# Two exponent operations and three rounding operations moved later in the first head pair of a fused attention and feed-forward kernel

## The chip, the cores and the metric

One core of one Trainium2 chip. The time is the device time of one execution in microseconds (us). Executions of one kernel scatter by 1 to 2 us here, so small differences are judged on several runs beside runs of the kernel before on the same chip.

Engines by their short names: PE is TensorE (matmuls), PEld its weight loads, DVE VectorE, ACT ScalarE, POOL GpSimd, SP SyncE, which issues most loads. L171 is line 171 of the kernel.

## The reference

Attention with a hashed mask over 4 x 8 heads of 768 positions and 64 features, followed by a feed-forward block on the result. Cut to what matters:

```python
q_bits = (np.einsum('bhsd,dk->bhsk', q, proj) > 0)      # likewise k_bits
mask = q_bucket[:, :, :, None] == k_bucket[:, :, None, :]
scores = np.where(mask, scale * q @ k.T, -1e9)
attn = softmax(scores) ; x = attn @ v                    # (cut, in words)
h = x @ w_in ; r = np.maximum(h, 0) ; out = (r * r) @ w_out
```

The two weights of the feed-forward block arrive in float64 (a float32 array times a float64 scalar). The kernel has to make float32 of them itself, and does so with integer operations, 512 columns of 128 rows at a time, between the steps of the attention. Such a chunk is called a piece; each pair of heads brings two.

## The kernel before

Heads are worked off in 16 pairs. For a pair, PE makes hash values of 64 features, ACT turns them into bits, PE makes scores for six tiles of keys, ACT their exponentials, DVE adds these up, and PE multiplies them with the values ("attend"). A piece of weights needs three steps on two engines:

```python
    def part_weight(i):                     # splitting, on DVE: L143, L147
        nc.vector.tensor_scalar(out=power, in0=high, ...)
        nc.vector.tensor_scalar(out=top, in0=high, ...)

    def place_power(i):                     # exponent operations, on ACT: L160, L161
        nc.scalar.activation(out=small, in_=power, func=ACTF.Relu, bias=excess)
        nc.scalar.activation(out=power, in_=small, func=ACTF.Copy, scale=2.0**23)

    def round_weight(i):                    # rounding, on DVE: L171, L176, L179
        nc.vector.scalar_tensor_tensor(out=power, in0=high, ..., in1=power, ...)
        ...                                 # two more of the same kind
```

The first of the three rounding operations reads what the second exponent operation wrote. The loop over pairs, cut to the steps that the argument touches, in program order. Each engine gets its own instructions in this order:

```python
        for pr in range(NP):
            a, b = 2 * pr, 2 * pr + 1       # the two pieces of this pair
            ...
            if more and pr > 0:
                for w in range(2):
                    features(pr + 1, w)     # DVE: transposes q and k of the next pair, L333
            if pr > 0:
                round_weight(b - 2)
            ...
            score(pr, 0); score(pr, 1)      # PE: scores; ACT: exponentials
            if pr > 0:
                finish(pr - 1, prepare if more else None)   # PE: next pair's hash (L346),
                                            # sums of the last (L455), attends, spread (L477)
            add_up(pr, 1)                   # DVE
            ...
            part_weight(a)
            score(pr, 2)
            if pr == 0:
                prepare()                   # hash and bits of pair 1
            score(pr, 3)
            ...
            place_power(a)
            attend(pr, 0); attend(pr, 1)
            for kt in (2, 3):
                add_up(pr, kt)              # DVE
            ...
            round_weight(a)
            part_weight(b)
            ...
            score(pr, 4); score(pr, 5)
            if pr == 0:
                weigh(1)                    # ACT: L382
            place_power(b)
            attend(pr, 2); attend(pr, 3)
            add_up(pr, 4); add_up(pr, 5)    # DVE
```

Scores, hashes and sums share three buffers of PE's output memory. So the fourth user in a row has to wait until the first one has been read.

## Time and profile before

| | before |
|---|---|
| time, median of the 6 runs at the change's measurement | 880.06 us (879.69 to 881.27) |
| PE busy, share of the span | 99% |
| DVE busy | 87% |
| PE idle in 21 to 26 us | 1.37 of 5.00 us |
| PE's wait for tile 4's exponential | 0.99 us |
| hash of pair 2 on PE | 1.48 us |

The profile prints a group of instructions on a line: start, length, engine, line and operation, what it writes and reads, how often, and in brackets what ended an idle time before it. Lines the prediction shows are not repeated. These are PE's in the first pair and at pair 2's hash, in the timeline of the kernel before:

```profile
22.99 0.40 PE L396 MATMUL st<-bits,bits 64*128 64x512 bf16 x2
23.20 1.04 PE L396 MATMUL st<-feat,feat 64*128 64x512 f32 x4
25.23 0.29 PE L396 MATMUL st<-bits,bits 64*128 64x256 bf16 x2 [0.99 <-ACT e L413]
...
31.44 0.60 PE L396 MATMUL st<-feat,feat 64*128 64x256 f32 x4
31.96 1.48 PE L346 MATMUL hash<-feat,projs 64*32 64x384 f32 x16
33.37 0.85 PE L455 MATMUL tot<-total,ones 128*32 128x384 f32 x8
...
36.79 0.26 PE L477 MATMUL xo<-both,picks 128*64 128x24 f32 x4
```

The bracket at 25.23 is the wait that the change is after. The hash at 31.96 starts without a gap behind the scores of 31.44, but lasts 1.48 us. The line at 36.79 is a handy milestone further on.

### The profile page before, as it was taken

What the parts mean: (1) busy time and instruction counts of PE and PEld (TensorE: products, weight loads), DVE (VectorE), ACT (ScalarE), POOL (GpSimd) and SP (SyncE); (2) the same over time, 40 slices, a digit from 0 to 9 for tenths busy, and PEclk for the clock granted to TensorE, in tenths of its full rate; (3) what the DMA queues carried; (4) which work ended last, traced back from release to release, by engine and by line L of the source; (5) the groups of instructions that cost most, each with busy time, mean ns of one, the idle gap of its engine ahead of it and who ended that gap; (6) DMA issues with size and microseconds to landing.
All of it is one profiled execution on the core that took longest, in us unless ns stands there. A gap on an engine that the chain in (4) does not pass through costs nothing.

```text
span 877.9 us, 12130 instructions
## 1 busy us (share of the span) xinstructions
PE 864.8 (99%) x4340; PEld 518.7 (59%) x4340; DVE 760.4 (87%) x1099; ACT 391.5 (45%) x673; POOL 107.0 (12%) x172
## 2 busy tenths in 40 slices
PE   8999999999999999999999999999999999999996
PEld 3444444444444444444688865556888755568885
DVE  5999999999999998888779968888889788888875
ACT  6988888888888852222211123332111233321110
POOL 2000000000000001554231011111000211110002
PEclk9999999999999999999999999999999999999998
DMA  9777967998788536999897764536756754355565
GB/s 176 142 149 134 233 153 156 188 253 225 179 176 225 156 105 213 299 267 283 292 353 239 181 160 168 173 118 222 285 151 187 167 165 155 124 167 154 158 175 105
DMA packets 224131, 167.09 MB, mean 190 GB/s; under 512 B 164448, under 2 KB 181344, under 8 KB 224064
## 3 DMA queue, kind: packets, MB, share of 16 engines
q1 hardware_dynamic: 189152, 87.19, 41.0%
q0 software_dynamic: 12528, 41.30, 15.2%
q10 hardware_dynamic: 22384, 37.76, 14.0%
q8 instruction: 36, 0.59, 0.3%
q14 instruction: 31, 0.25, 0.1%
HBM read 124.52 MB, written 41.68 MB: 189 GB/s over the span
## 4 chain that ended last, share of the span: by engine, by line
PE 95%; DVE 2%; ACT 1%; DMA 1%; issue 0%; ACTq 0%; DVEq 0%
PE acc L712 40%; PE st L396 17%; PE acc L931 16%; PE xo L438 14%; PE acc L884 6%; PE hash L346 2%; PE tot L455 1%; DVE total L428 1%; DMA k_nat<-in_k_dram 1%; ACT bits L356 1%; ACT e L413 0%; PE xo L477 0%; DVE x_t L493 0%; PE tp L309 0%; DVE recs L487 0%
## 5 line engine op out<-in xcount | busy, mean ns | idle before, releaser
L413 ACT ACTIVATE e<-st 128x1024 f32<-128x1024 f32 x192 | 145.1, 810 | 44.9 <-PE st L396 41.0
L396 PE MATMUL st<-feat,feat 64*128 64x512 f32 (+1 forms) x768 | 150.4, 483 | 0.0
L438 PE MATMUL xo<-e,v_nat 128*64 128x512 f32 (+1 forms) x768 | 134.8, 492 | 0.0
L712 PE MATMUL acc<-b,leaf 128*128 128x256 f32 x600 | 133.2, 379 | 0.7 <-issue 0.7
L712 PEld LDWEIGHTS acc<-b,leaf 128*128 128x128 f32 x600 | 113.8, 190 | 17.1 <-issue 1.7
L428 DVE TENSOR_TENSOR total<-total,e 128x1536 f32<-128x1536 f32 x64 | 112.4, 1757 | 8.2 <-ACT e L413 3.6
L438 PEld LDWEIGHTS xo<-e,v_nat 128*64 128x64 f32 x768 | 51.3, 136 | 82.2 <-issue 74.3
L931 PE MATMUL acc<-t_x,w_unit 128*128 128x512 f32 x192 | 90.2, 592 | 0.0
L396 PEld LDWEIGHTS st<-feat,feat 64*128 64x128 f32 x768 | 66.0, 188 | 33.0 <-issue 23.2
L712 PE MATMUL acc<-t,leaf 128*128 128x256 f32 x336 | 76.3, 380 | 0.0
L356 ACT ACTIVATE bits<-hash,lifts 32x384 bf16<-32x384 f32 x120 | 68.6, 572 | 2.3 <-PE hash L346 0.5
L712 PEld LDWEIGHTS acc<-t,leaf 128*128 128x128 f32 x336 | 63.6, 190 | 9.4 <-DVE t L516 0.5
L796 DVE SCALAR_TENSOR_TENSOR b<-h 128x512 f32<-128x512 f32 x96 | 65.7, 691 | 3.0
L396 PE MATMUL st<-bits,bits 64*128 64x256 bf16 (+1 forms) x384 | 63.1, 325 | 1.7 <-ACT e L413 1.2
L931 PE MATMUL acc<-x,w_unit 128*128 128x512 f32 x128 | 60.1, 592 | 0.0
L712 PE MATMUL acc<-x,w_unit 128*128 128x512 f32 x128 | 56.6, 594 | 0.0
L712 PE MATMUL acc<-b_t,leaf 128*128 128x256 f32 x240 | 53.8, 379 | 0.0
L931 PEld LDWEIGHTS acc<-t_x,w_unit 128*128 128x128 f32 x192 | 36.5, 190 | 28.9 <-issue 26.8
L719 ACT COPY two<-acc 128x256 f32<-128x256 f32 (+1 forms) x29 | 12.5, 431 | 87.9 <-PE acc L712 63.1
L719 ACT COPY one<-acc 128x256 f32<-128x256 f32 (+1 forms) x29 | 12.5, 431 | 85.1 <-PE acc L712 46.9
L712 PEld LDWEIGHTS acc<-b_t,leaf 128*128 128x128 f32 x240 | 45.5, 190 | 6.2
L396 PEld LDWEIGHTS <-bits 64*128 64x128 bf16 x384 | 23.5, 93 | 42.5 <-issue 38.4
(159 smaller groups left out, 1165.5 us busy)
## 6 DMA issues: line engine op xcount, KB each, us to landing
leaf<-w_out ACTq DMA_DIRECT2D x142, 256.0 KB, 3.1
w_unit<-w_in SPq DMA_DIRECT2D x16, 640.0 KB, 4.0
raw<-in_moe_w_in_dram SPq DMA_DIRECT2D x16, 512.0 KB, 5.6
raw<-in_moe_w_out_dram SPq DMA_DIRECT2D x16, 512.0 KB, 4.6
w_unit<-w_in SPq DMA_DIRECT2D x8, 896.0 KB, 8.1
w_out<-sums POOLq DMA_DIRECT2D x16, 448.0 KB, 6.8
sum<-w_in SPq DMA_DIRECT2D x16, 448.0 KB, 4.8
v_nat<-in_v_dram SPq DMA_DIRECT2D x16, 384.0 KB, 4.3
```

The costliest lines, as they stand in the source:

```text
L346: nc.tensor.matmul(out=banks[g * NR_B:(g + 1) * NR_B, h, 0:HS], lhsT=projs[rows], rhs=feat[pr, w][rows, c * HS:(c + 1) * HS], start=True, ...
L356: nc.scalar.activation(out=t[h * D:h * D + NR_B, c * HS:(c + 1) * HS], in_=hashed[pr, w][at, h, 0:HS], func=ACTF.Sign, scale=HUGE, bias=li ...
L396: nc.tensor.matmul(out=st[:, h, 0:hi - lo], lhsT=src[pr, 1][rows, key], rhs=src[pr, 0][rows, lo:hi], start=first, stop=not first,)
L413: nc.scalar.activation(out=e[:, :, lo:hi], in_=sts[i][:, :, 0:hi - lo], func=ACTF.Exp, scale=scale)
L428: nc.vector.tensor_tensor(out=totals[pr], in0=totals[pr], in1=weights[pr, kt][:, :, 0:S], op=ALU.add)
L438: nc.tensor.matmul(out=xo[h * D:(h + 1) * D, lo:hi], lhsT=nat[pr, "v_nat"][:, h, kt * D:(kt + 1) * D], rhs=weights[pr, kt][:, h, lo:hi], s ...
L455: nc.tensor.matmul(out=tot[g * 32:(g + 1) * 32, 0:HS], lhsT=ones, rhs=totals[pr][:, h, c * HS:(c + 1) * HS], start=True, stop=True,)
L712: nc.tensor.matmul(out=acc[to], lhsT=a(i), rhs=b(i), start=first and i == 0, stop=last and i == n - 1, skip_group_check=True,)
L719: nc.scalar.copy(out=t, in_=acc[of])
L796: nc.vector.scalar_tensor_tensor(out=out, in0=h, scalar=0.0, in1=h, op0=ALU.max, op1=ALU.mult)
L884: nc.tensor.matmul(out=out, lhsT=w[:, a], rhs=b, start=start, stop=stop, skip_group_check=True)
L931: nc.tensor.matmul(out=acc[to], lhsT=w[:, PLACE[a], f], rhs=bt[b](f), start=first and f == 0, stop=last and f == NFT // 2 - 1, skip_group_ ...
```

## The change

In the first pair the exponent operations of piece 0 stand ahead of the exponentials of tiles 4 and 5, which PE waits for. The change puts them behind those exponentials, and the rounding, which needs them, behind that. Other pairs are untouched. The whole diff:

```diff
             score(pr, 3)
             if more and pr > 0:
                 weigh(pr + 1)
-            place_power(a)
+            if pr > 0:
+                place_power(a)
             attend(pr, 0)
             attend(pr, 1)
@@
-            round_weight(a)
+            if pr > 0:
+                round_weight(a)
             part_weight(b)
@@
             score(pr, 5)
             if pr == 0:
                 weigh(1)
+                place_power(0)
+                round_weight(0)
             place_power(b)
             attend(pr, 2)
             attend(pr, 3)
```

## The prediction

> **What bounds the kernel now.** I read the page first: busy shares, slices and the chain of waits. Then I read the change's own place, the first pair of heads, in the timelines of ScalarE (ACT), VectorE (DVE) and TensorE (PE), and last the busy time by stretch, to see whether anything lost early can be won back. From the page, the busy shares, three of the forty slices' rows, and the chain by engine:
>
> ```profile
> PE 864.8 (99%) x4340; PEld 518.7 (59%) x4340; DVE 760.4 (87%) x1099; ACT 391.5 (45%) x673; POOL 107.0 (12%) x172
> ...
> PE   8999999999999999999999999999999999999996
> ...
> DVE  5999999999999998888779968888889788888875
> ...
> PEclk9999999999999999999999999999999999999998
> ...
> PE 95%; DVE 2%; ACT 1%; DMA 1%; issue 0%; ACTq 0%; DVEq 0%
> ```
>
> PE sets the time: 95% of the chain. A microsecond that PE stands still in the attention stage ends in the time, unless a later stall would have absorbed it. The busy time by stretch says whether there is one (columns: stretch, length, then busy PE, weight loads, DVE, ACT, POOL):
>
> ```profile
> 21.00:26.00 5.00, 3.63 (x26) 1.95 (x27) 3.08 (x4) 4.92 (x8) 0.00 (x0) 1.00 0.99 221
> ...
> 34.00:54.00 20.00, 20.00 (x152) 9.13 (x148) 18.83 (x23) 17.00 (x26) 0.00 (x0) 1.00 0.71 133
> 54.00:74.00 20.00, 20.00 (x154) 9.17 (x150) 18.56 (x22) 17.16 (x26) 0.00 (x0) 1.00 0.70 132
> ```
>
> From 34 us on PE is busy 20.00 of 20 us; there is no later stall to absorb anything. Its only idle time near the change lies in 21 to 26 us, where ACT is busy 4.92 of 5.00. DVE has about 1.2 us of slack per 20 us. The chain of waits in that place:
>
> ```profile
> 21.34 1.51 ACT e L413 x2
> 22.86 0.03 issue
> 22.88 0.73 ACT small L160
> 23.61 0.02 issue
> 23.64 0.63 ACT power L161
> 24.27 0.93 ACT e L413
> 25.19 0.04 issue
> 25.23 0.72 PE st L396 x6
> ```
>
> Here the two exponent operations (L160, L161, of weight piece 0) stand ahead of the exponentials of key tile 4, and PE waits for the first of those. That is the wait the change aims at. The work that the change will displace is seen on DVE:
>
> ```profile
> 22.89 1.76 DVE L428 TENSOR_TENSOR total<-total,e 128x1536 f32<-128x1536 f32 x1 [3.59 <-ACT e L413]
> 24.57 0.69 DVE L171 SCALAR_TENSOR_TENSOR power<-raw,power 128x512 uint32<-128x512 uint32 x1
> ...
> 26.50 0.42 DVE L143 TENSOR_SCALAR power<-raw 128x512 uint32<-128x512 uint32 x1
> ...
> 27.17 3.62 DVE L428 TENSOR_TENSOR total<-total,e 128x1536 f32<-128x1536 f32 x2
> 30.70 0.97 DVE L333 STREAM_TRANSPOSE feat<-q_nat 128x768 f32<-128x768 f32 x1
> 31.60 0.94 DVE L333 STREAM_TRANSPOSE feat<-k_nat 128x768 f32<-128x768 f32 x1
> ```
>
> DVE idles 3.59 us, but only until 22.89; from there it runs without a gap through rounding of piece 0 (24.57), splitting of piece 1 (26.50), two additions (27.17) and the transposes of pair 2 (30.70, 31.60). PE already waits for the last of these: its weight load for the second half of the hash has "[0.47 <-DVE feat L333]" at 32.59. The hash of pair 2 takes PE 1.41 us in the chain, that of pair 3 only 0.81, so DVE is already 0.6 us late there.
>
> **What the Trainium skill says.** "Perfetto Trace Analysis", section "Tensor Engine Instruction (MATMUL, LD_WEIGHTS)": ACT and DVE are strict FIFO; only PE can pull weight loads ahead. So a DVE instruction that waits for ACT holds up everything behind it on DVE. The trace agrees: the timelines of both keep the program's order throughout, and DVE's 3.59 us wait was spent with the additions for tile 3 at the head. "ScalarE: Activation LUTs", section "What ACT_TABLE_LOAD costs": back-to-back ACTIVATEs overlap by about 93 ns. The trace agrees (the exponential of 1.025 us at 21.34 is followed 0.92 us later by the next), so I count from start to start. "TensorE: Matmul & The Clock Gate", section "What's actually happening": after an idle window of about 3.4 us the PE clock falls to half. The trace before has no such gap in this stage and shows clock 1.00; I use it below as a rival.
>
> **The change, part by part.** Nothing is added or removed: two ACT operations and three DVE operations of piece 0 move. All figures are estimates from starts in the timelines.
>
> (a) ACT. The exponential of tile 4 starts at 22.88 instead of 24.17, 1.29 us earlier. The four exponentials of tiles 4 and 5 and the hand-over to the weighing took 26.93 - 24.17 = 2.76 us, back to back, and their scores come in time, so weighing (L382) starts at about 25.65. Then L160 of piece 0 follows 0.83 later (27.76 - 26.93), at 26.48; L161 0.76 later, at 27.24; it ends at 27.87 (0.63). Before, it ended at 24.27. Piece 1 follows, and ACT is free for the next pair's exponentials at about 29.1.
>
> (b) PE, the gain. The second cut of tile 5's scores started at 25.23, behind the exponential. Without the wait it follows its first cut by 1.09 us, as elsewhere (28.62 to 29.71): 22.99 + 1.09 = 24.08. Gain 1.15 us. PE runs the attends and the first scores of pair 1 that much earlier (28.62 becomes 27.47). Pair 1's first exponential begins at about 29.1 and frees its buffer at 30.15, about when PE asks for it (31.33 - 1.15 = 30.18), so at most a few hundredths are lost. PE reaches pair 2's hash at 31.96 - 1.15 = 30.81.
>
> (c) DVE, the cost. After the addition at 22.89, DVE next splits piece 1 at 24.57 (0.67 us, from 27.17 - 26.50), done at 25.24. At the head now stands the rounding of piece 0, which needs L161's result: 27.87 plus 0.03 (the gap seen at 43.67) = 27.90. DVE idles 2.66 us. Rounding takes 26.50 - 24.57 = 1.93, so the additions start at 29.83 instead of 27.17, 2.66 us late. The two transposes, with no idle between, start 2.66 us late too: 33.36 and 34.26.
>
> (d) PE, the loss. The hash needs these transposes. Its second half started at 32.59, 0.05 behind the end of the key transpose, and now starts at 35.25. The 1.15 us of (b) turn into waiting, since PE arrives at 30.81 and finds no features until about 34.4. From the hash on, PE, ACT and DVE all have the same distances as before, shifted by 2.66 us: rounding of piece 1 and the transposes of the sums stand the same way behind the hash.
>
> Sum: gain (b) 1.15, all of it swallowed in front of the hash; DVE's delay 3.33 (27.90 against 24.57) less 0.67 of splitting done in the gap = 2.66 us lost for good. 880.21 + 2.66 = 882.87, say 882.9 us, 0.3% more.
>
> **The rivals.**
> 1. The intended effect alone: PE's stall goes and DVE does not matter; -1.15 us, 879.1. For it: 3.59 us of idle on DVE just ahead, and ACT's wait is really in the chain. Against it: that idle lies before 22.89, so it can't be used, and PE already waits for the key transpose at 32.59. DVE would have to be nearly 3 us ahead there; it is behind.
> 2. DVE makes the delay good: it has 1.2 us of slack per pair. That helps DVE, not PE: the stall happens at the very next hash, before any slack comes, and PE never has a gap afterwards in which to recover. This would leave +1 to +2 us, 881 to 882, if PE's arrivals elsewhere are less tight than I read them.
> 3. The clock: PE's wait of 34.4 - 30.8 = 3.6 us is close to the skill's window. If the clock halves until PE has been busy for another window, the 3 to 4 us after the hash stretch, an estimated 1.7 to 2 us: 884.7. The window isn't aligned with my gap and the first half of the hash falls inside the later part, so I give it about 1 in 7.
> 4. A transfer: piece 3's load needs piece 0's raw buffer, which the rounding frees at about 29.2; it was issued at 29.84 anyway. Hidden, no change.
>
> **Range and chances.** The three runs before span 1.3 us. The loss of 2.66 rests on one edge (ACT to DVE to hash) with a tenth or two of error; rival 3 gives the upper tail, rival 2 the lower. Predicted 882.9, eight in ten within 881.4 to 885.0. A change of 2% would be 17.6 us, six times everything moved here: within 2% 0.985, slower 0.01, faster 0.005.
>
> **What would show it.** (a) L160 of piece 0 at about 26.5 behind L382. (b) No wait of 0.99 us ahead of tile 5's second cut. (c) A new wait of about 2.7 us on DVE ahead of L171, released by "ACT power L161", and the additions at 29.8. (d) A wait of about 3.6 us on PE ahead of the hash, "DVE feat L333", the hash's second half at 35.25, and from there every start about 2.7 us later than before. Busy time unchanged on all engines but for a PE clock below 1.00 if rival 3 holds. It would be wrong if the additions of tiles 4 and 5 or the transposes ran ahead of the rounding on DVE, if the hash didn't wait for the transposes, or if later starts didn't keep the shift.

## The result, and the profile after

The changed kernel took 884.64 us in the median of 6 runs (882.99 to 885.57); the kernel before 880.06. The ratio is 1.0047, with a 95% interval of 1.0034 to 1.0060: slower by half a per cent, clear of noise, and within 2%. The median lies in the predicted range of 881.4 to 885.0, 1.7 us above the predicted 882.9.

DVE's timeline of the changed kernel, from the addition of tile 3 to the transposes of pair 2:

```profile
22.86 1.76 DVE L428 TENSOR_TENSOR total<-total,e 128x1536 f32<-128x1536 f32 x1 [3.61 <-ACT e L413]
24.54 0.42 DVE L143 TENSOR_SCALAR power<-raw 128x512 uint32<-128x512 uint32 x1
...
28.09 0.69 DVE L171 SCALAR_TENSOR_TENSOR power<-raw,power 128x512 uint32<-128x512 uint32 x1 [2.77 <-ACT power L161]
...
30.03 3.54 DVE L428 TENSOR_TENSOR total<-total,e 128x1536 f32<-128x1536 f32 x2
33.49 0.97 DVE L333 STREAM_TRANSPOSE feat<-q_nat 128x768 f32<-128x768 f32 x1
34.38 0.94 DVE L333 STREAM_TRANSPOSE feat<-k_nat 128x768 f32<-128x768 f32 x1
```

The new wait is the bracket at 28.09: 2.77 us with nothing to do, released by the second exponent operation. From there to the transposes DVE runs without a gap and late: the key transpose at 34.38 instead of 31.60, 2.78 us. ACT released it late because the exponent operations now stand behind the weighing (L382), as its timeline shows:

```profile
25.85 0.94 ACT L382 ACTIVATE bits<-bits,gains 128x768 bf16<-128x768 bf16 x1
26.69 0.71 ACT L160 ACTIVATE small<-power,excess 128x512 uint8<-128x512 uint32 x1
27.43 0.63 ACT L161 ACTIVATE power<-small 128x512 uint32<-128x512 uint8 x1
```

PE's timeline of the changed kernel:

```profile
23.17 1.04 PE L396 MATMUL st<-feat,feat 64*128 64x512 f32 x4
24.03 0.29 PE L396 MATMUL st<-bits,bits 64*128 64x256 bf16 x2
...
30.41 0.61 PE L396 MATMUL st<-feat,feat 64*128 64x256 f32 x4
34.60 2.27 PE L346 MATMUL hash<-feat,projs 64*32 64x384 f32 x16 [3.58 <-DVE feat L333]
36.81 1.51 PE L455 MATMUL tot<-total,ones 128*32 128x384 f32 x8
38.24 3.97 PE L438 MATMUL xo<-e,v_nat 128*64 128x512 f32 x16
42.05 0.25 PE L477 MATMUL xo<-both,picks 128*64 128x24 f32 x4
```

The wait at 25.23 is gone: that matmul starts at 24.03, 1.20 us earlier. Then PE stands for 3.58 us ahead of the hash. And the hash, the sums and the attends, which have the same work as before, are slower: the sums take 1.51 us instead of 0.85. The milestone comes at 42.05 instead of 36.79, 5.26 us late. That is 2.78 from the transposes and 2.48 from something else.

The busy time by stretch shows what. Its columns are the stretch and its length, the busy time of PE, PEld, DVE, ACT and POOL with their instructions, the granted clock of PE as a share of full speed, and the DMA's share and rate. The stretches are cut where the clock record has its steps:

```profile
30.39:33.80 3.41, 0.63 (x6) 0.22 (x5) 3.38 (x3) 1.74 (x3) 0.00 (x0) 1.00 0.88 196
33.81:37.21 3.40, 2.61 (x20) 0.63 (x24) 3.37 (x5) 0.27 (x1) 0.00 (x0) 0.50 0.00 0
37.23:40.63 3.40, 3.40 (x16) 0.97 (x10) 2.11 (x4) 3.31 (x7) 0.00 (x0) 0.50 0.02 5
40.64:44.00 3.36, 3.36 (x29) 1.78 (x28) 2.14 (x3) 1.44 (x3) 0.00 (x0) 1.00 0.00 0
```

The granted clock was 0.50 from 33.8 to 40.6, 6.83 us long, and 1.00 before and after. From there to the end of the attention stage PE's instructions keep their distance: matched one by one, the starts of the two kernels differ by 5.25 us all the way from 37 us to 334. In the feed-forward block behind it the distance falls to 5.0 and at the end to 4.6 us; there other pairs of kernels drift by some tenths too (e2 goes from 0.16 us late to 0.47 early against the kernel before).

One view misleads here. The chain of waits of the changed kernel, in the place where PE stands:

```profile
29.81 3.64 DMA raw<-in_moe_w_in_dram
33.45 0.04 issue
33.49 0.98 DVE feat L333
```

It leads through the load of a weight piece which landed at 33.45 by chance. The transposes read no weights, and DVE's timeline shows them directly behind the additions, without idle time. In the kernel before the same load was issued at 29.84 and the transposes ran at 30.70.

### The profile page after: what moved, and what is told of

The parts are those of the page before. It is cut to its first block, busy times and chain, and to the rows that moved or that the text cites. A ratio compares the mean times of both kernels' runs of the same rounds, so it can differ in the third digit from the quotient of the medians.

```text
span 882.6 us, 12133 instructions
## 1 busy us (share of the span) xinstructions
PE 867.5 (98%) x4340; PEld 520.6 (59%) x4340; DVE 760.0 (86%) x1099; ACT 391.5 (44%) x673; POOL 107.0 (12%) x172
## 4 chain that ended last, share of the span: by engine, by line
PE 95%; DVE 2%; SPq 1%; DMA 1%; issue 0%; ACT 0%; DVEq 0%
PE acc L716 40%; PE st L396 16%; PE acc L935 16%; PE xo L438 13%; PE acc L888 5%; PE hash L346 2%; PE tot L455 1%; SPq L287 1%; DVE total L428 1%; DMA w_in<-s_in 1%; PE xo L326 0%; DMA raw<-in_moe_w_in_dram 0%; PE tp L309 0%; SPq L130 0%; PE xo L477 0%
## 5 line engine op out<-in xcount | busy, mean ns | idle before, releaser
L396 PEld LDWEIGHTS st<-feat,feat 64*128 64x128 f32 x768 | 66.0, 188 | 32.9 <-issue 22.9
```

Source lines behind the costliest of these rows:

```text
L396: nc.tensor.matmul(out=st[:, h, 0:hi - lo], lhsT=src[pr, 1][rows, key], rhs=src[pr, 0][rows, lo:hi], start=first, stop=not first,)
```

## The experiments

Every kernel was run in five rounds (e10 gave six runs). The diffs of e2, e3, e6 and e7 are against the kernel before, the others against the changed kernel. Two theories were tested together. First, DVE's wait at the head of its queue is passed on one to one through the transposes and the hash. Second, PE's stand then drops its clock. The kernel before had medians of 879.6 to 880.1 in all of them.

**e1: keep PE's clock up.** Into the changed kernel, 48 idle matmuls ahead of pair 2's hash, into columns of its buffer that are not used. The result stays right.

```diff
-                hash_bits(pr + 1, turn("hash"))
+                banks = turn("hash")
+                if pr == 1:
+                    for _ in range(48):
+                        nc.tensor.matmul(out=banks[:, 0, HS:512], lhsT=busy[:, 0:P],
+                                         rhs=busy[:, 0:128], start=True, stop=True)
+                hash_bits(pr + 1, banks)
```

> The changed kernel with 48 idle matmuls (128 columns, bf16, into unused columns of the hash buffer) placed on TensorE in front of pair 2's hash, where it stands still. Theory (two costs: VectorE's delay of about 2.7 us, and on top of it, in some runs, the TensorE clock halved for 6.8 us after a stand of 3.6 us): the clock record shows no half-clock stretch after the start, every run lies at 882.7 to 883.3, mean clock 0.996, none at 884 to 886. Rival (the extra 1.3 to 2.6 us of four of six runs come from something else that the change disturbs, such as the transfers): still 884 to 886 in most runs, the filler changes nothing. Second rival (the wait on VectorE is not the cause of the rest): with the clock kept up the time falls below 882.

882.34 us (881.76 to 883.49), ratio 1.0031. The median is 0.4 us under the expected band, and the runs scatter wider than it; one of five lies under the second rival's 882. No half-clock stretch stands in its record; the same place in its busy time by stretch:

```profile
32.00:36.00 4.00, 3.27 (x46) 1.70 (x47) 4.00 (x5) 0.09 (x1) 0.00 (x0) 1.00 0.21 80
36.00:42.00 6.00, 6.00 (x46) 2.82 (x40) 5.76 (x10) 5.81 (x10) 0.00 (x0) 1.00 0.00 0
```

The DVE wait was 2.78 us as in the changed kernel. The key transpose and the milestone:

```profile
34.00 0.94 DVE L333 STREAM_TRANSPOSE feat<-k_nat 128x768 f32<-128x768 f32 x1
...
39.19 0.26 PE L477 MATMUL xo<-both,picks 128*64 128x24 f32 x4
```

Against the kernel before the transpose is 2.40 us late and the milestone is 2.40 us late. (In e12, the same kernel again, 2.77 and 2.76. These differ by what the kernels scatter at the start, some 0.2 us.) So with the clock kept up nothing is left beyond DVE's delay, and the 2.48 us of "something else" are gone. That answers the first rival, the transfers, and the second.

**e2: the rounding's move alone.** Exponent operations at their old place, rounding behind the splitting of piece 1.

```diff
-            round_weight(a)
+            if pr > 0:
+                round_weight(a)
             part_weight(b)
@@
                 weigh(1)
+                round_weight(0)
             place_power(b)
```

> Only one part of the change: in pair 0 the rounding of piece 0 stands behind the splitting of piece 1, the two exponent operations stay where they were before. Theory (the loss comes from VectorE waiting for ScalarE's late exponent operation, not from the order of VectorE's own work): no wait of VectorE in front of the rounding, pair 2's transposes start at 30.7 and 31.6 as before, 880.1 within 0.4 us. Rival (a later rounding costs by itself, by holding its raw buffer or by its place): 881 or more.

879.63 us (878.98 to 880.91), ratio 0.9999 (0.9985 to 1.0012). DVE ran from splitting to rounding without idle time. The order of DVE's own work costs nothing; the rival falls.

**e3: an ill-made run.** Meant as the exponent operations' move alone, with the rounding left ahead.

```diff
-            place_power(a)
+            if pr > 0:
+                place_power(a)
@@
                 weigh(1)
+                place_power(0)
             place_power(b)
```

> The other part alone: piece 0's exponent operations behind the last exponentials and the weighing, its rounding at the old place. Theory: VectorE waits for ScalarE from 24.5 to 28.1, then rounds, and only then splits piece 1, so the second transposes of pair 2 end about 0.67 us later than in the changed kernel; the hash's second half at about 36.0, a loss of about 3.4 us against before: 883.5 with the clock up, up to 886.5 where it falls. Rival (moving the exponent operations off the exponentials' way is the gain that was meant, and the rounding's move is what costs): 879 to 880.

880.20 us (879.20 to 880.64), ratio 1.0001, and a wrong result (relative error 0.28). The expectation is void. In the program the rounding came first and took the piece off the list, so `place_power(0)` found nothing to do and the two operations were never made. What ran is therefore another experiment: the two exponent operations taken away altogether. It still says something. Its PE timeline:

```profile
23.89 0.29 PE L396 MATMUL st<-bits,bits 64*128 64x256 bf16 x2
...
31.65 1.62 PE L346 MATMUL hash<-feat,projs 64*32 64x384 f32 x16 [0.96 <-DVE feat L333]
```

PE's wait in tile 5 was gone, a gain of 1.34 us at that matmul against before. But PE then stood 0.96 us ahead of the hash, because DVE's transposes were no earlier, and the time did not move. Even for free, the gain that was meant ends at the hash as long as DVE's work in front of the transposes is the same.

**e4: the rounding behind the transposes.** The changed kernel, with piece 0's rounding in pair 1.

```diff
                 place_power(0)
-                round_weight(0)
@@
             if more and pr > 0:
                 for w in range(2):
                     features(pr + 1, w)
+            if pr == 1:
+                round_weight(0)
             if pr > 0:
                 round_weight(b - 2)
```

> The changed kernel, but with piece 0's rounding taken out from in front of the additions of tiles 4 and 5 and put behind pair 2's transposes. Theory (only the rounding's place at the head of VectorE costs; the gain on TensorE of 1.15 us is real and was swallowed): VectorE starts the additions at about 25.2 and pair 2's transposes at about 28.8 and 29.7, TensorE does not wait for them, no clock fall; TensorE gains 1.2 us and loses the 0.6 us of the old wait too, gives some back when pair 0's sums wait behind two roundings: 878.6 to 879.7, faster than the kernel before. Rival (the two exponent operations ahead of pair 1's exponentials cost by delaying ScalarE): 880.5 or more, with TensorE waiting for an exponential of pair 1.

878.83 us (878.48 to 879.17), ratio 0.9987 (0.9973 to 1.0000). Its PE timeline:

```profile
31.14 0.88 PE L346 MATMUL hash<-feat,projs 64*32 64x384 f32 x16
...
35.83 0.30 PE L477 MATMUL xo<-both,picks 128*64 128x24 f32 x4 [0.30 <-DVE both L466]
```

The hash starts without a wait and takes 0.88 us, and only 0.30 us are given back behind the two roundings. The exponent operations stand exactly where the change put them. So it is the rounding, waiting for its late input in front of the additions and transposes, that costs. With the rounding out of the way the move on ACT costs nothing, and with its input ready (e2) the rounding's move costs nothing either.

**e5: the exponent operations' move alone, made properly.** Rounding ahead of the splitting of piece 1, as before the change.

```diff
-            part_weight(b)
+            if pr > 0:
+                part_weight(b)
@@
                 round_weight(0)
+                part_weight(1)
             place_power(b)
```

> Replaces the ill-made run e3: piece 0's exponent operations behind the last exponentials and the weighing, its rounding still ahead of the splitting of piece 1 as before the change. Theory (VectorE waits for ScalarE at the head of its queue and all behind it is late by the same): VectorE waits about 3.5 us, from 24.5 to 28.1, the splitting no longer fills part of that wait, so pair 2's key transpose ends 0.67 us later than in the changed kernel, the hash's second half at about 36.0 against 32.6 before; 883.5 where the clock stays up, 885 to 887 where it falls. Rival (once the exponent operations are behind the exponentials TensorE has its 1.15 us and the rest is overlap): 880.5 or less.

884.72 us (883.97 to 886.05), ratio 1.0057. DVE waited 3.47 us, and the hash's second half started at 36.23. PE stood in two parts, 2.54 us for an exponential of pair 1 and 1.20 us ahead of the hash, and the clock fell all the same. Two of the five times lie in the band for a fallen clock, three up to 1.0 us under it.

**e6 and e7: the kernel before with DVE made late on purpose.** One and two useless additions ahead of pair 2's transposes; the difference is the count in `range`.

```diff
+    idle = const.tile([P, 2, S], FP32, name="idle")      # and a memset on GpSimd
@@
+            if pr == 1:
+                for _ in range(1):                       # e7: range(2)
+                    nc.vector.tensor_tensor(out=idle[:, :, 0:S], in0=idle[:, :, 0:S],
+                                            in1=idle[:, :, 0:S], op=ALU.add)
             if more and pr > 0:
                 for w in range(2):
                     features(pr + 1, w)
```

> The kernel before, with one useless addition (128x1536 fp32) on VectorE ahead of pair 2's transposes; nothing else moves. Theory (each microsecond by which those transposes are late is a microsecond of time, none is made good): start to start such an addition takes 1.68 us, so 1.68 us over before, 881.7; TensorE stands 1.4 us ahead of the hash, no clock fall. Rival (VectorE's slack of about 1.2 us per later pair makes the delay good): 880.6 or less.

> The same with two useless additions. Theory: 3.36 us over before in every run, 883.4; TensorE stands about 3.1 us ahead of the hash, a little under the 3.6 of the changed kernel, so the clock falls in few runs or none; where it does, 1.3 to 2.6 us more. If the clock fell in most runs as in the changed kernel, the length of the stand would not be what decides. Rival (the delay is made good later): 881.5 or less, the two doses not in proportion.

e6: 881.95 us (881.74 to 882.55), ratio 1.0024, 1.85 us over before in the median where 1.68 was expected; PE stood 1.46 us ahead of the hash and the mean clock was 0.996 or more in all runs. e7: 885.16 us (883.24 to 885.94), ratio 1.0057. Two of its runs, of mean clock 0.997 and 0.998, took 883.24 and 883.28, 3.2 us over before as against 3.36 expected. The three others, of 0.994 and 0.995, took 885.16 to 885.94. PE's stand was 3.26 us in the profiled run, one of the two with the clock up. In the profiles the key transpose of pair 2 is 1.64 and 3.63 us later than in the kernel before, and the milestone 1.64 and 3.62; both distances stand to within 0.01 us up to 333 us. So DVE's delay passes on one to one for the two doses, and the slack of later pairs makes nothing good. The expectation that the clock would fall in few runs or none missed: by the mean clocks it fell in three of five, though none of these was profiled.

**e8 and e10: the order that the runs point to.** Exponent operations as in the change; piece 1 split in DVE's idle time before 22.9; piece 0 rounded after pair 0 is normalised. e10 is the same kernel again.

```diff
             part_weight(a)
+            if pr == 0:
+                part_weight(b)
             score(pr, 2)
@@
-            part_weight(b)
+            if pr > 0:
+                part_weight(b)
@@
                 place_power(0)
-                round_weight(0)
@@
                 normalize(pr - 1)
+            if pr == 1:
+                round_weight(0)
```

> The order the runs point to: exponent operations of piece 0 behind the last exponentials as in the change, but piece 1 split ahead of the addition of tile 3, in VectorE's idle time before 22.9, and piece 0 rounded only after pair 0 has been normalised. Theory: TensorE keeps the 1.15 us, does not wait for pair 2's transposes, and does not wait 0.3 us for pair 0's sums as in e4; 878.3 to 879.0, at or a little under e4's 878.8. Rival (what is moved later on VectorE returns as a wait at pair 3's hash): 879.5 to 880.2.

> The order of e8 again, unaltered: is it reliably under the kernel before? Theory: 878.3 to 879.5 with before at 880, ratio about 0.9987. If e8 was only favourable scatter: 879.6 to 880.3.

e8: 878.93 us (878.14 to 879.62), ratio 0.9988 (0.9974 to 1.0002). e10: 878.78 us (878.47 to 879.27), ratio 0.9987 (0.9974 to 0.9999). They are 1.2 and 1.1 us under the kernel before in their medians, and no better than e4, which is the simpler edit. It is a gain of a tenth of a per cent, at the edge of what these intervals can tell. The profiles speak for it: from pair 1 to the end of the attention stage DVE's normalising (L493) starts 0.83 to 0.92 us earlier than in the kernel before in all three (e4, e8, e10), where the kernels' starts scatter by some 0.2 us. All three beat the changed kernel by over 5 us.

**e9, e11 and e12: how often the clock falls, and what it costs.** e9 and e11 are the changed kernel unaltered, e12 is e1's kernel beside e11.

> The changed kernel unaltered, for a larger count of how often the TensorE clock falls. Theory (loss of VectorE's delay in every run, the clock on top in some): two groups of runs, those of mean clock 0.996 and more at 882.6 to 883.4, those of 0.995 and less at 884 to 886; the second group 2 to 5 of 5. Rival (one broad spread that the clock doesn't order): the times do not sort by the clock.

> The changed kernel unaltered, beside e12 on the same chip. In e9 two runs of mean clock 0.996 lay at 884.1, so the mean clock alone does not sort the runs; this pair tells the clock's part apart on one chip. Theory: 884.0 to 884.8.

> The filled kernel of e1 again, beside e11. Theory (the clock is what costs beyond VectorE's delay): 882.2 to 883.0, 1.3 to 2.2 us under e11, no half-clock stretch in its profile. Rival (e1's lower times were the chip's): within 0.7 us of e11.

e9: 884.29 us (884.09 to 884.64), ratio 1.0049. The expected two groups did not come out: three runs of mean clock 0.993 at 884.3 to 884.6 and two of 0.996 at 884.1 to 884.2. e11: 883.86 us (883.73 to 884.44), ratio 1.0049, in three of five runs just under what was expected, all runs at 0.995 or 0.996. Its profile explains the middle group:

```profile
31.98:35.38 3.40, 0.81 (x12) 0.23 (x15) 3.40 (x4) 0.12 (x1) 0.00 (x0) 1.00 0.20 81
35.39:38.79 3.40, 3.40 (x21) 0.63 (x20) 2.21 (x4) 1.86 (x4) 0.00 (x0) 0.50 0.02 5
38.80:42.00 3.20, 3.20 (x26) 1.58 (x24) 2.77 (x5) 2.71 (x5) 0.00 (x0) 1.00 0.00 0
```

Here the clock was halved for 3.41 us, half as long as in the first profile, and the milestone came at 41.11, 0.94 us earlier than there. So there are shorter and longer falls, and the record shows where they part: in all four profiles with a fall the clock came back after the first stretch of 3.41 us at half clock that was full of matmuls. In e11 that was the first one (3.40 us busy); in the changed kernel's first profile, in e5 and in e9 the first one held 2.61, 1.83 and 1.94 us, and a second one followed. e12: 882.86 us (882.08 to 883.11), ratio 1.0035, 1.0 us under e11 in the median and 1.3 in the mean, a little less than expected against an e11 in which the clock fell briefly. No run of e12 is as slow as the fastest of e11, on the same chip in the same rounds. The rival that e1's times were its chip's falls.

Three profiles of the unaltered changed kernel were taken (the first, e9, e11), and the clock fell in all three. For the other runs only the mean clock is known. The four profiled runs with a fall (e5's is the fourth) have 0.992, 0.993, 0.993 and 0.996, those without one 0.996 to 0.998. So values of 0.995 and under are taken here for a fall, which is an inference; 0.996 occurs with and without one, so for the two runs at 883.0 of the first measurement it stays open whether the clock fell briefly or not.

## Why the prediction was right or wrong

The time lay in the range, slower by a sum that the named mechanism gives. By its steps:

- **(a) ACT.** Right, 0.2 us too early: the first exponent operation started at 26.69 against 26.48 predicted. Tile 4's exponential did start a little sooner than said, at 22.71, but the way from there to the weighing took 3.14 us instead of 2.76: the short exponentials were followed after 0.6 to 0.7 us, not 0.48 as before, and tile 5's first began at 24.31, only when its scores were done.
- **(b) PE's gain.** Right: 1.20 us against 1.15, and wholly lost at the hash, as predicted. e3 shows it once more: with the operations taken away the time stays.
- **(c) DVE's wait.** Right: 2.77 us against 2.66; rounding at 28.09 against 27.90; transposes 2.78 us late against 2.66. e2 and e5 separate it: without the wait nothing is lost, and without the splitting in the gap the wait is 3.47.
- **(d) PE's loss, passed on without recovery.** Right in its edge: the stand ahead of the hash was 3.58 us against 3.6 predicted, the hash's second half started at 35.37 against 35.25, and every later start up to 334 us keeps its shift, which is 5.25 us where 2.66 was predicted; the rest is the clock's (below). The doses e6 and e7 show it in the other kernel.
- **The sum.** It has the term that was mis-sized. The prediction put the clock's halving outside the sum, at "about 1 in 7", and so counted nothing for it in 882.9. It fell in all three profiles and, by the mean clocks, at least in four of the six first runs. Its cost was 2.48 us at the milestone in the first profile, 2.1 us in e9's and 1.6 us in e11's (milestones 5.26, 5.11 and 4.32 us late, less the transposes' 2.78, 2.97 and 2.74), and 1.3 to 1.8 us in the mean between filled and unfilled kernels (882.50 and 882.72 against 884.04 to 884.33). The size given for the case that it falls, 1.7 to 2 us and 884.7, is near what came, 884.64. That it is so near is partly luck: the same kernel's medians in e9 and e11 were 884.29 and 883.86. That the range held, although 882.9 was missed by 1.7 us, is owed to its upper end, which was given to this rival.
- **Why the chance was mis-sized.** The prediction reasoned that a whole window of 3.4 us had to be idle, which a stand of 3.6 us rarely covers. The record lets one find the windows: the falls begin 8 or 9 times 3.41 us behind the clock record's first step (27.31 us in the first profile, e5 and e9, 30.72 in e11), and last once or twice 3.41. The windows before them were not idle: 0.63 us of matmuls in the first profile, 0.81 in e11 with the hash already running. In e5 and e9 the clock fell after one with 1.25 and 1.28 us, while e7's profile, with 1.44 us in one, shows no fall:

```profile
29.22:32.63 3.41, 1.25 (x8) 0.48 (x5) 3.37 (x5) 1.94 (x3) 0.00 (x0) 1.00 1.23 149
32.64:36.04 3.40, 1.83 (x10) 0.76 (x13) 3.38 (x3) 2.25 (x4) 0.00 (x0) 0.50 0.57 155
```

These two lines are e5's busy time by stretch, cut at the clock's steps. The next is e7's; it has no step there, so the stretch is cut by the count of 3.41 us from its record's first step:

```profile
30.75:34.15 3.40, 1.44 (x12) 0.55 (x8) 3.37 (x3) 2.35 (x4) 0.00 (x0) 1.00 1.04 198
```

Every other window counted so in the first 45 us of the fourteen profiles, at full clock, holds 2.1 us or more. So a stand need not fill a window. An estimate from these numbers: wherever a stand of 3.58 us falls on windows of 3.41, one of them is left with less than 1.28 to 1.44 us of matmuls in 8 to 9 positions of 10, and without any in 1 of 20.

- **The rivals.** The intended gain alone (879.1) and DVE making it good (881 to 882) both fell. The load of piece 3 was issued at 29.81 against 29.84 before, hidden as said. The clock, rival 3, came true.

What stays open: how little activity in a window makes the clock fall, which these five profiles put between 1.28 and 1.44 us of matmuls if matmul time is what counts, and whether e8 is truly better than e4.

## What to carry to other kernels

An operation moved off one engine's critical place takes its dependents with it: look at who stands behind the dependent on its own in-order engine, and place it behind whatever the bottleneck needs next (e4), not merely behind its producer. Idle time of an engine counts as slack only if it lies between the new wait and the work that the bottleneck needs next. And when a change makes PE stand for some 3 us, reckon with a clock penalty of half the loss to nearly the whole of it (1.6 to 2.5 us on 2.7 to 3.0 here), and keep PE busy if the stand can't be avoided.

## What the Trainium skill lacked or had wrong

- "TensorE: Matmul & The Clock Gate", section "What's actually happening", has the clock fall after at least one idle window of about 3.4 us. The length agrees (half-clock stretches of 3.41 and 6.83 us), but the window need not be empty of matmuls: the clock fell after windows of 3.41 us with 0.63, 0.81, 1.25 and 1.28 us of them, and not after one with 1.44. The section doesn't say how little activity counts as idle.
- The same page, section "HAM oscillation — how this bites in real kernels", gives the rule of no PE idle gaps over about 3.4 us. That is too lax: stands of 2.54 and 1.20 us in near succession (e5) sufficed, and in e7, whose profiled run stood 3.26 us and kept its clock, mean clocks of 0.994 and 0.995 point to falls in three of five runs.
- "Perfetto Trace Analysis", section "Tensor Engine Instruction (MATMUL, LD_WEIGHTS)", calls DVE and ACT strict FIFO; that held, and the 2.77 us on DVE is what it costs. What follows from it, and no page spells out, is that idle time before a new wait is of no use to it: 3.61 us of idle ended at 22.86, and 2.77 us of new idle began at 25.3.
